# Moving the last stores of a long convolution's first stage to the SP queue, and two group loads behind its last direct transfers

## The chip, the cores and the metric

The kernel runs on one core of one Trainium2 chip. The metric is the time of one execution on the device in microseconds (us). Three runs took 2814.12, 2816.59 and 2818.91 us; the median is 2816.59 us.

## The reference

Three parts follow each other. The first is a long causal convolution by FFT of `u = x * v` (2 sequences of 12480 positions, 128 channels) with a filter that a small two-layer network makes from position embeddings, times `x`. The second and third are two expert layers over the 24960 rows, with hidden width 2048.

```python
h_filt = (np.maximum(pos_emb @ w1, 0.0) @ w2) * window
u = x * v
y = irfft(rfft(u, n=2*S) * rfft(h_filt, n=2*S), n=2*S)[:, :S]
x = (x * y).reshape(B * S, 128)
x = np.square(np.maximum(x @ w_in, 0)) @ w_out        # first expert layer
h = x @ w2_in;  out = (h * np.cos(h)) @ w2_out        # second expert layer
```

## The kernel before, in words

The FFT is written as two rounds of matrix products with a turned layout between them. That gives three stages.

**First stage** (`NCH` = 30 chunks, q = 0 to 29, each of two pairs i = 0, 1). SP loads chunk q in one transfer of 1360 KB (`load`, line 155) into one of five slots. PE multiplies by the first table (`pair`, line 198), ACT copies one half out (`v`, line 200), and DVE makes sum and difference into the tile `bt` (line 202). `store(q)` writes `bt` of both pairs to the DRAM tensor `Bs` (line 205), on the ACT queue: 112 rows of 12288 bytes, 1344 KB. In the same loop `decode` prepares the expert weights on DVE, ACT and POOL, from loads `wr` (line 84) on the SP queue.

**Second stage** (`NG` = 26 groups, g = 0 to 25). Group g needs 120 rows of `B2[g]`, one for each pair of spectrum lines; chunk q of the first stage makes rows 4q to 4q+3 of every group. `load2(g, a, b)` (line 134, on SP) reads rows a to b-1 of group g from `Bs`; each row is four pieces of 3072 bytes, one for each of the four values of k that belong to the group. A whole `load2(g)` has 128 rows (1536 KB). Only the `Bs` rows k = 4g to 4g+3 are read, so for groups 0 to 3 the first 16 rows of a store are enough. That is why the last stores are cut in two, `slice(0, 16)` (192 KB) and `slice(16, NP)` (1152 KB). `NB` = 3 groups have a slot at a time, and these slots are three of the five that the chunks used.

Rows of group 0 that come from the last two chunks don't go through DRAM: `direct(q)` (line 212) copies them inside SBUF with four transfers of 12 KB, each from 4 rows of `bt` to one row of `B2[0]`. Transfers n = 0, 1 need the first pair, n = 2, 3 the second.

PE starts a group with `spectrum` (line 285, tile `H`), two products with the filter part, one for each of c = 0, 1; ACT turns `H` into `hi` and `hr` (lines 288 to 292). Then come `product` (line 307, tile `Z`), the elementwise products on DVE and POOL, and the inverse products (line 342). In the order of the program PE does H(0,0), H(0,1), then Z of group 0's first half, then H(1,0) of group 1, then Z of group 0's second half, then H(1,1), and so on: the first product of group g+1 stands in the middle of group g, on PE and on ACT.

**Third stage.** The rest of the convolution and both expert layers, in 50 blocks of up to 512 rows.

Every engine and every queue takes its instructions in the order of the program, written out by hand. A DMA is issued when its data, its buffer, and one of eight completion semaphores are free; the semaphores are dealt out in turn, so a DMA also waits for the landing of the eighth DMA before it.

Of the kernel before, what the change touches and what calls it, by code (L numbers as in the profile page):

```python
# [23 lines left out]
NP = 112  # L24
NCH, CB = 30, 2
# [12 lines left out]
NB = 3  # L38
BT = 3
R = 96  # L40
# [14 lines left out]
def conv_moe(ctx, tc, t):  # L55
    nc = tc.nc
# [61 lines left out]
    def decode(n):  # L118
        for _ in range(n):
            next(steps, None)  # L120
# [6 lines left out]
    def slot(name, pool=ring, size=SLOT):  # L127
        return pool.tile([128, size], F32, tag="ld", name=name)

    def load2(g, a=0, b=128):  # L130

        if g not in B2:
            B2[g] = slot("B2").rearrange("p (k c e) -> p k c e", k=G4, c=2)
        nc.sync.dma_start(out=B2[g][a:b].rearrange("p k c e -> p k (c e)"),
                          in_=bass.AP(Bs.tensor, G4 * g * 4 * HB * 384 + 768 * a,
                                      [[768, b - a], [4 * HB * 384, G4], [1, 768]]))


    with ExitStack() as st:
# [37 lines left out]
        def prep(q, i):  # L177
            _, xt, vt, _ = ld[q]
            if i == 0:
                ut_t[q] = io.tile([NP, CB, 2, 384], F32, tag="ut", name="ut", bufs=3)  # L180
            u = ut_t[q]
            nc.gpsimd.tensor_tensor(out=u[:, i, :, 0:256], in0=xt[:, i], in1=vt[:, i], op=ALU.mult)
            hp = psM.tile([128, 2 * D], F32, tag="m", name="hp2")[0:NP].rearrange("p (a d) -> p a d", a=2)
            nc.tensor.matmul(hp, hT_t[q][:, i, :], w2b, start=True, stop=True)
            for a in range(2):
                nc.scalar.activation(u[:, i, a, 256:384], hp[:, a, :], AF.Copy, scale=win[:, q, i, a:a + 1])
# [3 lines left out]
        def pair(q, i):  # L190
            if i == 0:
                bt_t[q] = io.tile([NP, CB, 2, 2, 384], F32, tag="bt", name="bt", bufs=BT)
            u, bt = ut_t[q], bt_t[q]
            A = {}
            for a in (1, 0):
                A[a] = psA.tile([NP, 2, 512], F32, tag="A", name="A")
                for r in range(2):
                    nc.tensor.matmul(A[a][:, r, 0:384], turned(q, i, a, r), u[:, i, a, :], start=True, stop=True)
            v = wk.tile([NP, 2, 384], F32, tag="v", name="v")
            nc.scalar.activation(v, A[1][:, :, 0:384], AF.Copy)  # L200
            for c, op in ((0, ALU.add), (1, ALU.subtract)):
                nc.vector.tensor_tensor(out=bt[:, i, :, c, :], in0=A[0][:, :, 0:384], in1=v, op=op)

        def store(q, rows=slice(0, NP), eng=nc.scalar):
            eng.dma_start(out=Bs[rows, 8 * q:8 * (q + 1), :].rearrange("k x e -> k (x e)"),
                                in_=bt_t[q][rows].rearrange("k b r c e -> k (b r c e)"))

        def direct(q):

            for n in range(2 * CB):  # L210
                eng = nc.scalar if n % 2 else nc.sync
                eng.dma_start(out=B2[0][2 * CB * q + n:2 * CB * q + n + 1].rearrange("p k c e -> p (k c e)"),
                              in_=bt_t[q][0:G4, n // 2, n % 2].rearrange("k c e -> k (c e)"))

# [5 lines left out]
        def upto(kind, fn, n, end):  # L220
            while done[kind] < min(n, end):
                fn(done[kind])
                done[kind] += 1
# [4 lines left out]
        for n, (q, i) in enumerate(seq):  # L228
            lead = min(LA, n + 1) if n else 1
            upto("mlp", mlp1, (n + lead - 1) // CB + 1, NCH)  # L230
            upto("prep", lambda m: prep(*seq[m]), n + lead, len(seq))
            pair(q, i)
            upto("mlp", mlp1, (n + lead + 1) // CB + 1 if n else 1, NCH)
            if i == 0 and 0 < q < NCH - 2:
                store(q - 1)
            if i == 0 and q >= NCH - 4 and q - NCH + 4 < NB:
                load2(q - NCH + 4, 0, R)
            if i == 0 and q >= NCH - 2:
                store(q - 1, slice(0, 16))
                if q == NCH - 2:  # L240
                    load2(0, R, 2 * CB * q)
                else:
                    direct(q - 1)
                store(q - 1, slice(16, NP))
            if (q, i) == (NCH - 1, 1):
                direct(q)
                store(q, slice(0, 16))
                for g in range(1, NB):
                    load2(g, R)
                store(q, slice(16, NP))  # L250
            if i == 1:
                upto("load", load, q + LDB + 1, NCH)
            if 1 < n < WS:
                decode(2)
# [479 lines left out]
```

## Time and profile before

| | |
|---|---|
| median of three runs | 2816.59 us (2814.12 to 2818.91) |
| the profiled execution | 2814.05 us |
| its span from first to last instruction | 2812.3 us |
| PE / ACT / DVE / POOL busy in the span | 97% / 86% / 85% / 48% |
| chain that ended last | PE 80%, DVE 1%, ACT 1% |
| second stage begins on PE | at 254.19 us |

The page counts an engine as busy while it works on data; issuing DMAs, waiting and branching are not counted. The DMA share is the mean busy share of the core's 16 DMA engines. PEclk is the granted clock of TensorE as a share of full speed. `SPq` and `ACTq` are the instructions with which SP and ACT issue DMAs: their times are those of the issue, not of the transfer.

### The profile page before, as it was taken

What the parts mean: (1) busy time and instruction counts of PE and PEld (TensorE: products, weight loads), DVE (VectorE), ACT (ScalarE), POOL (GpSimd) and SP (SyncE); (2) the same over time, 40 slices, a digit from 0 to 9 for tenths busy, and PEclk for the clock granted to TensorE, in tenths of its full rate; (3) what the DMA queues carried; (4) which work ended last, traced back from release to release, by engine and by line L of the source; (5) the groups of instructions that cost most, each with busy time, mean ns of one, the idle gap of its engine ahead of it and who ended that gap; (6) DMA issues with size and microseconds to landing.
All of it is one profiled execution on the core that took longest, in us unless ns stands there. A gap on an engine that the chain in (4) does not pass through costs nothing.

```text
span 2812.3 us, 38640 instructions
## 1 busy us (share of the span) xinstructions
PE 2740.5 (97%) x11740; PEld 2107.4 (75%) x11740; DVE 2388.5 (85%) x4675; ACT 2416.4 (86%) x4292; POOL 1353.7 (48%) x1049
## 2 busy tenths in 40 slices
PE   8887999899999999999999999999999999999999
PEld 4543444788888888888888888888888888888887
DVE  5786999788888888888888888888888888888888
ACT  4444999699999999999999999999999999999998
POOL 4554888144444444444444444444444444444445
PEclk9999999999999999999999999999999999999999
DMA  9997887310101100101110001010001011001000
GB/s 376 391 391 260 275 284 253 90 29 25 31 28 31 28 29 19 32 28 31 28 31 19 29 28 31 28 31 28 20 27 32 28 32 28 23 25 32 16 9 9
DMA packets 83257, 222.53 MB, mean 79 GB/s; under 512 B 5552, under 2 KB 49160, under 8 KB 75848
## 3 DMA queue, kind: packets, MB, share of 16 engines
q1 hardware_dynamic: 78689, 177.99, 19.9%
q10 hardware_dynamic: 4359, 42.08, 3.7%
q8 instruction: 92, 1.51, 0.2%
q14 instruction: 117, 0.96, 0.1%
HBM read 140.29 MB, written 79.63 MB: 78 GB/s over the span
## 4 chain that ended last, share of the span: by engine, by line
PE 80%; DVE 1%; ACT 1%; issue 0%; DMA 0%; POOL 0%; SPq 0%; DVEq 0%; ACTq 0%; POOLq 0%
PE h L489 13%; PE h L491 13%; PE h L490 13%; PE y L505 13%; PE y L503 13%; PE y L504 13%; PE pc L455 4%; DVE g L577 0%; DVE r L562 0%; ACT k L554 0%; DMA dt<-dt 0%; DVE gh L587 0%; ACT g L534 0%; ACT c L569 0%; ACT r L528 0%
## 5 line engine op out<-in xcount | busy, mean ns | idle before, releaser
L594 POOL TENSOR_TENSOR gl<-g,gh 128x512 fp32r<-128x512 f32 (+2 forms) x800 | 1034.5, 1293 | 1279.9 <-ACT gh L585 738.4
L577 DVE TENSOR_TENSOR g<-h,c 128x512 f32<-128x512 f32 (+2 forms) x800 | 539.8, 675 | 244.9 <-ACT c L569 238.2
L489 PE MATMUL h<-zh,wh 128*128 128x512 f32 (+2 forms) x1600 | 642.8, 402 | 0.8 <-DVE zh L473 0.8
L554 ACT ACTIVATE k<-h,quarter 128x512 int32<-128x512 f32 (+2 forms) x800 | 541.7, 677 | 114.0 <-PE h L491 99.9
L505 PE MATMUL y<-gl,wh 128*128 128x512 f32 (+2 forms) x1600 | 624.8, 391 | 3.6 <-POOL gl L594 2.1
L491 PE MATMUL h<-zh,wl 128*128 128x512 f32 (+2 forms) x1600 | 623.4, 390 | 0.0
L490 PE MATMUL h<-zl,wh 128*128 128x512 f32 (+2 forms) x1600 | 623.1, 389 | 0.0
L503 PE MATMUL y<-gh,wl 128*128 128x512 f32 (+2 forms) x1600 | 622.6, 389 | 0.1
L504 PE MATMUL y<-gh,wh 128*128 128x512 f32 (+2 forms) x1600 | 622.1, 389 | 0.0
L569 ACT ACTIVATE c<-r,halfpi 128x512 f32<-128x512 f32 (+2 forms) x800 | 565.2, 706 | 2.6 <-DVE r L562 2.6
L528 ACT ACTIVATE r<-h 128x512 f32<-128x512 f32 (+2 forms) x800 | 472.0, 590 | 95.2 <-PE h L491 94.9
L548 DVE TENSOR_TENSOR gl<-g,gh 128x512 fp32r<-128x512 f32 (+2 forms) x800 | 537.5, 672 | 1.2
L562 DVE CUSTOM_DVE_ANT_0 r<-h,k 128x512 f32<-128x512 f32 (+2 forms) x800 | 537.8, 672 | 0.0
L534 ACT ACTIVATE g<-r 128x512 f32<-128x512 f32 (+2 forms) x800 | 492.2, 615 | 0.7 <-DVE gl L548 0.2
L541 DVE CAST gh<-g 128x512 fp32r<-128x512 f32 (+2 forms) x800 | 333.1, 416 | 41.2 <-ACT g L534 38.8
L505 PEld LDWEIGHTS y<-gl,wh 128*128 128x128 f32 x1600 | 301.4, 188 | 75.0 <-POOL gl L594 7.5
L503 PEld LDWEIGHTS y<-gh,wl 128*128 128x128 f32 x1600 | 301.7, 189 | 67.4 <-DVE zl L516 0.6
L491 PEld LDWEIGHTS h<-zh,wl 128*128 128x128 f32 x1600 | 302.0, 189 | 66.6
L504 PEld LDWEIGHTS y<-gh,wh 128*128 128x128 f32 x1600 | 301.6, 188 | 66.5
L489 PEld LDWEIGHTS h<-zh,wh 128*128 128x128 f32 x1600 | 302.7, 189 | 58.1 <-issue 1.0
L490 PEld LDWEIGHTS h<-zl,wh 128*128 128x128 f32 x1600 | 302.5, 189 | 56.3
L585 ACT ACTIVATE gh<-g 128x512 fp32r<-128x512 f32 (+2 forms) x400 | 246.4, 616 | 0.1
(62 smaller groups left out, 2439.4 us busy)
## 6 DMA issues: line engine op xcount, KB each, us to landing
ld<-ld SPq DMA_DIRECT2D x30, 1360.0 KB
Bs<-bt ACTq DMA_DIRECT2D x27, 1344.0 KB
B<-Bs SPq DMA_DIRECT2D x23, 1536.0 KB
Ds<-dt SPq DMA_DIRECT2D x26, 960.0 KB
dt<-Ds SPq DMA_DIRECT2D x59, 416.0 KB
xt<-xT SPq DMA_DIRECT2D x60, 208.0 KB
out<-o SPq DMA_DIRECT2D x47, 256.0 KB
tt<-T SPq DMA_DIRECT2D x60, 169.0 KB
```

Of the source, the lines that this page charges most:

```text
L489: nc.tensor.matmul(h[:, :n], wh[:, f, :], zh[:, :n], start=True, stop=False)
L490: nc.tensor.matmul(h[:, :n], wh[:, f, :], zl[:, :n], start=False, stop=False)
L491: nc.tensor.matmul(h[:, :n], wl[:, f, :], zh[:, :n], start=False, stop=True)
L503: nc.tensor.matmul(y[:, :n], wl[:, f, :], gh[:, :n], start=a, stop=False)
L504: nc.tensor.matmul(y[:, :n], wh[:, f, :], gh[:, :n], start=False, stop=False)
L505: nc.tensor.matmul(y[:, :n], wh[:, f, :], gl[:, :n], start=False, stop=b)
L548: nc.vector.tensor_tensor(out=gl[:, :n], in0=g[:, :n], in1=gh[:, :n].bitcast(F32), op=ALU.subtract)
L554: nc.scalar.activation(k[:, :n], hp[2, u][:, :n], AF.Identity, scale=-1.0, bias=quarter)
L562: nc.vector._custom_dve(TENSOR_ADD_SAT, out=r[:, :n], in0=h[:, :n], in1=k[:, :n], s0=0.25, s1=-0.75)
L569: nc.scalar.activation(c[:, :n], r[:, :n], AF.Sin, bias=halfpi, scale=TWO_PI)
L577: nc.vector.tensor_tensor(out=g[:, :n], in0=h[:, :n], in1=c[:, :n], op=ALU.mult)
L594: nc.gpsimd.tensor_tensor(out=gl[:, :n], in0=g[:, :n], in1=gh[:, :n].bitcast(F32), op=ALU.subtract)
```

## The change

The stores of chunks 25 to 28 and the first 16 rows of chunk 29 are issued by SP and no longer by ACT. Of the groups, only group 0 is loaded early; rows 0 to 95 of groups 1 and 2 are no longer loaded at chunks 27 and 28. After the last `direct`, group 1 is loaded as rows 0 to 115 and rows 116 to 127, and group 2 in one piece. The transfers of `direct(28)` are all on SP; those of `direct(29)` alternate between SP and ACT as before. Rows 96 to 111 of group 0 are loaded one pair later, at (28, 1), and `direct(28)` stands ahead of the stores of chunk 28.

```diff
         def direct(q):
             for n in range(2 * CB):
-                eng = nc.scalar if n % 2 else nc.sync
+                eng = nc.scalar if q == NCH - 1 and n % 2 else nc.sync
...
-            if i == 0 and 0 < q < NCH - 2:
+            if i == 0 and 0 < q < NCH - 4:
                 store(q - 1)
-            if i == 0 and q >= NCH - 4 and q - NCH + 4 < NB:
-                load2(q - NCH + 4, 0, R)
+            if i == 0 and NCH - 4 <= q < NCH - 2:
+                store(q - 1, eng=nc.sync)
+                if q == NCH - 4:
+                    load2(0, 0, R)
             if i == 0 and q >= NCH - 2:
-                store(q - 1, slice(0, 16))
-                if q == NCH - 2:
-                    load2(0, R, 2 * CB * q)
-                else:
+                if q == NCH - 1:
                     direct(q - 1)
-                store(q - 1, slice(16, NP))
+                store(q - 1, slice(0, 16), nc.sync)
+                store(q - 1, slice(16, NP), nc.sync)
+            if (q, i) == (NCH - 2, 1):
+                load2(0, R, 2 * CB * q)
             if (q, i) == (NCH - 1, 1):
                 direct(q)
-                store(q, slice(0, 16))
-                for g in range(1, NB):
-                    load2(g, R)
+                store(q, slice(0, 16), nc.sync)
+                load2(1, 0, 2 * CB * q)
+                load2(1, 2 * CB * q)
                 store(q, slice(16, NP))
+                for g in range(2, NB):
+                    load2(g)
```

## Rows read from the trace of the kernel before

**Rows 1.** Stages: stretch, its length, busy time (count) by engine, granted clock, DMA share, GB/s.

```profile
200.00:242.00 42.00, 37.35 (x116) 20.90 (x116) 36.31 (x48) 17.28 (x35) 19.65 (x15) 0.96 0.99 362
242.00:254.00 12.00, 0.48 (x2) 0.00 (x0) 2.16 (x3) 0.81 (x1) 1.31 (x2) 0.73 0.84 228
300.00:450.00 150.00, 147.08 (x333) 60.61 (x332) 138.42 (x217) 138.21 (x234) 125.01 (x100) 1.00 0.88 284
600.00:700.00 100.00, 100.00 (x452) 81.89 (x451) 86.56 (x177) 91.44 (x159) 44.97 (x34) 1.00 0.08 22
```

**Rows 2.** Order of time, 225 to 300 us: start, length, engine, line, idle before and its releaser.

```profile
234.46 2.23 PEld L198 LDWEIGHTS A<-ut,ld 112*112 112x112 f32 x8 [0.35 <-POOL ut L182]
236.12 0.81 ACT L200 ACTIVATE v<-A 112x768 f32<-112x768 f32 x1 [1.78 <-PE A L198]
...
238.20 1.81 DVE L202 TENSOR_TENSOR bt<-A,v 112x768 f32<-112x768 f32 x2
239.63 2.22 PEld L198 LDWEIGHTS A<-ut,ld 112*112 112x112 f32 x8 [0.36 <-issue]
240.53 1.82 DVE L202 TENSOR_TENSOR bt<-A,v 112x768 f32<-112x768 f32 x2
243.43 0.81 ACT L200 ACTIVATE v<-A 112x768 f32<-112x768 f32 x1 [3.91 <-DMA Bs<-bt]
244.27 1.82 DVE L202 TENSOR_TENSOR bt<-A,v 112x768 f32<-112x768 f32 x2 [1.93 <-ACT v L200]
254.19 3.73 PE L285 MATMUL H<-B,Gt 120*128 120x512 f32 x4 [11.71 <-DMA B<-bt]
262.24 1.13 PE L285 MATMUL H<-B,Gt 120*128 120x512 f32 x2 [2.60 <-ACT hr L292]
265.88 0.59 ACT L288 ACTIVATE hi<-H 64x512 f32<-64x512 f32 x1
271.87 1.02 PE L285 MATMUL H<-B,Gt 120*128 120x512 f32 x2
```

**Rows 3.** DMA issues in order of time, SP's and ACT's, each from its own stretch.

```profile
218.16 21.26 SPq L134 DMA_DIRECT2D B<-Bs  x4
239.12 0.30 SPq L134 DMA_DIRECT2D B<-Bs  x1
239.51 0.75 SPq L212 DMA_DIRECT2D B<-bt  x1
250.91 1.25 ACTq L212 DMA_DIRECT2D B<-bt  x2
252.21 0.92 ACTq L205 DMA_DIRECT2D Bs<-bt  x2
256.24 1.94 SPq L134 DMA_DIRECT2D B<-Bs  x2
```

**Rows 4.** Waits of the SP queue, 180 to 300 us: total, times, longest.

```profile
SPq L212 <- DMA B<-Bs: 7.6, 2, 4.3
```

**Rows 5.** DMA packets, 268 to 274.1 us: one whole `load2` of 128 rows alone.

```profile
DMA packets 529, 1.59 MB, mean 261 GB/s; under 512 B 16, under 2 KB 16, under 8 KB 528
q1 hardware_dynamic: 528, 1.57, 75.4%
```

**Rows 6.** DMA packets, 493 to 496.57 us: the end of one store of 120 rows.

```profile
DMA packets 174, 0.66 MB, mean 185 GB/s; under 512 B 15, under 2 KB 15, under 8 KB 172
```

**Rows 7.** DMA packets, 532 to 535.04 us: one load `tt` of 104 rows alone.

```profile
DMA packets 117, 0.17 MB, mean 57 GB/s; under 512 B 13, under 2 KB 117, under 8 KB 117
```

**Rows 8.** DMA packets, 252.2 to 252.95 us: direct transfers of 4 pieces.

```profile
DMA packets 8, 0.01 MB, mean 16 GB/s; under 512 B 4, under 2 KB 4, under 8 KB 8
```

**Rows 9.** DMA queue SP, 271 to 273 us: pieces of 3072 bytes, steady.

```profile
q1 hardware_dynamic: 272, 0.84, 102.8%
```

**Rows 10.** DMA queue SP, 243 to 245 us: pieces of 3072 bytes, crowded.

```profile
q1 hardware_dynamic: 145, 0.44, 100.3%
```

**Rows 11.** DMA queue ACT, 256 to 257 us: pieces of 12288 bytes of a store.

```profile
q10 hardware_dynamic: 32, 0.39, 109.7%
```

## The prediction

> **What bounds the kernel now.** I read the table of stages first, then the order of time around the border of stage one, then the DMA issues and SP's waits, and last the DMA packets of single transfers, because the change is about what the DMA engines do in which order.
>
> The stages have different limits [rows 1]. From 200 to 242 us the DMA engines are busy for 0.99 of the time, and no compute engine reaches 0.9. From 300 to 450 ACT (138.2 of 150) and PE (147.1) are nearly full, and the DMA engines have room. From 600 on PE is busy without a gap. So time gained or lost between stages one and two is not won back or hidden later: it goes to the end, one to one. The border itself is 242 to 254: 12 us in which PE works 0.48 us.
>
> Why 12 us? The last `bt` is ready at 244.27 + 1.82 = 246.09, and PE starts H(0,0) at 254.19 on the landing of a `direct` [rows 2]. Between them stands DMA queueing: the last two directs are issued by ACT from 250.91 to 252.16 [rows 3], not at 246.1; SP's directs waited 7.6 us for `B<-Bs` loads to land [rows 4]. Four such loads are issued between 218.16 and 239.42 [rows 3]; two of them are the early rows of groups 1 and 2, 1152 KB each. The last `v` also came late: it waited 3.91 us behind a store whose issue ACT could not finish before an earlier store had landed [rows 2].
>
> **The change, part by part.**
>
> *ACT loses its stores.* A `v` starts 236.12 - 234.46 = 1.66 us after PE's first weight load of its pair. For the last pair that gives 239.63 + 1.66 = 241.3 in place of 243.43. Then DVE is the next limit: it ends the `bt` before at 240.53 + 1.82 = 242.35, so the last one runs 242.4 to 244.2 in place of 246.09 [rows 2]. Gain 1.9 us.
>
> *The early loads of groups 1 and 2 go.* With them goes the wait of the directs for their landing. But SP now issues in one line: rows 96 to 111 of group 0 (after the first part of store 27), four directs at 0.75 us, the second two not before their `bt` at 238.20 + 1.81 = 240.0, the two parts of store 28, then two directs of chunk 29. The two waiting for 240.0 end at 241.4; the first part of store 28 goes out there, the second at 241.7. A small store took 256.24 - 252.21 = 4.0 us until the load that needs it was issued [rows 3], so it lands at 245.4. The second part has 96 rows, 6 for each engine; one row takes 1.097 x 16 / 32 = 0.55 us [rows 11], together 3.3 us. If it begins to move 1 us before the first part's landing is known (my estimate, from 0), it is through at 244.4 + 3.3 = 247.7.
>
> *The directs of chunk 29* are issued from 244.2 on (last `bt`), all four by 244.9. In the trace 2.6 us passed from the issue of the last direct, 251.6, to PE's start [rows 2, 3]; that alone would give 247.5. Two of the four stand on SP's queue behind store 28, through at 247.7; with about 1 us for landing and start, PE begins at 248.7. I take 248.5, which is 5.7 us earlier than 254.19; bounds 246.8 and 250.
>
> [...]
>
> *Group 1 is loaded late, and in an odd number of rows.* This is the step that decides. H(1,0) stands in PE's line after the first Z of group 0, and `hi` of group 1 in ACT's line. Before, PE reached it at 262.24, and ACT used it at 265.88, 265.88 - 254.19 = 11.7 us after the start [rows 2]. Started at 248.5, ACT comes to it at 260.2. By then rows 0 to 115 of group 1 must have landed.
>
> How fast are 116 rows? Each transfer closes with one small packet on each DMA engine that took part, and these are the packets under 512 bytes: 16 for a load of 128 rows [rows 5], 15 for 120 rows [rows 6], 13 for 104 rows [rows 7], 4 for a direct of 4 pieces [rows 8]. Each is the largest number up to 16 that divides the count of rows. For 116 = 4 x 29 that is 4. So I take 4 engines, each with 29 x 4 = 116 pieces of 3072 bytes. The nearest row counts, 104 and 120, ran on 13 and 15; on 15 engines each would have some 31 pieces. Those are the two ends, and I take 4 because the pattern fits all four rows.
>
> [...]
>
> One piece takes 1.028 x 16 x 2 / 272 = 0.121 us when the queue runs steadily [rows 9], 0.754 x 16 x 6.1 / 512 = 0.144 over a whole lone load with its start [rows 5], and 1.003 x 16 x 2 / 145 = 0.221 in the crowded stretch [rows 10]. With four engines asking instead of 16 I take the steady one: 116 x 0.121 = 14.0 us. The load is issued at 245.4 (it needs the first part of store 28) and moves on these engines when the store and the directs are through, at 248.1. The rest of store 29, on ACT's queue, shares them: 6 rows x 0.46 to 0.55, say 2.8 us. End: 248.1 + 14.0 + 2.8 = 264.9. Landing and start on PE 1 us, and H(1,0) at 1.9 us, because PE has stood idle again and runs slow: four products took 3.73 us at 254.19 after the long wait, two took 1.13 at 262.24 [rows 2]. ACT gets its first `hi` of group 1 at 267.8; before it was 265.88. Net: 1.9 us later.
>
> *Group 2 in one piece* follows on the same queue. Its 32 pieces for each engine take 3.9 us, so the four slow engines end at about 269. Before, H(2,0) came 271.87 - 262.24 = 9.6 us after H(1,0) [rows 2]; from 265.9 that is 275.5. Hidden, with 6 us to spare. The rows 96 to 111 of group 0 one pair later and store 25 and 26 on SP cost nothing: the DMA engines are full either way, and the load of group 0 is needed only with the last direct.
>
> *The sum*: -5.7 us at the start of stage two, and all of it plus 1.9 us is lost again in a new wait for group 1. Against the profiled execution's own 2814.05 us that is 2816.0; the median of the runs is 2.5 us above that execution, so 2818.5 on the median's scale. Bounds of the unknown: without the store in its way -2.8 + 1.9 = -0.9; at 0.144 us a piece 2.7 more, +4.6. Own range of the forecast 2815.5 to 2821.5.
>
> **The rivals.**
>
> *A. The load of 116 rows is spread over nearly all engines.* For it: 104 and 120 rows were. Then it takes about 32 pieces and lands before 256, group 1 is no wait, and the 5.7 us stay: 2816.6 - 5.7 = 2810.9. Against it: the pattern of small packets.
>
> *B. Slower than before: the four engines read at a crowded price.* The mechanism is the same new wait, with pieces that take longer, because their reads of DRAM meet the rest of store 29 and group 2. At 0.165 us a piece the price is 116 x 0.044 = 5.1 us more, 7.0 in all: 2823.6; at 0.221 it is 11.6 more, 2830.1. It decides from (5.6 - 1.9) / 116 = 0.032 above the steady price, 0.153 us, where the loss passes 0.2%. For it: the crowded stretch. Against: there 16 engines read at once, here four.
>
> *C. The directs gain nothing.* SP's single line holds them behind a store's landing, and PE starts as late as before or 2 us earlier; group 1's load then starts 3 to 4 us later too: +5.4, 2822. Against: the only landings in SP's line are those of store 27 and of the first part of store 28, and the second comes behind the directs.
>
> **How the numbers follow.** Forecast 0.62, A 0.13, B 0.17, C 0.08. About 0.2%, 5.6 us, is what a measurement can tell from no change: below 2811.0 faster, above 2822.2 slower. Faster: half of A (0.065) and an earlier start together with a cheap load, 0.065; 0.13. Slower: most of B (0.15), half of C (0.04) and the upper end of the forecast (0.07); 0.26. The same: 0.61. Range 2811 to 2825: it takes in A's time and the near half of B, and leaves out B beyond 0.18 us a piece.
>
> **What would show it.** In the trace after: the last `bt` ends near 244.2; PE's first `H` is at 247 to 250; then a second gap on PE of about 10 us, ended by `B<-Bs`; in that gap a DMA share near a quarter; 4 small packets at the end of the load of 116 rows. If PE has no second gap, the forecast is wrong and A holds. If the gap ends beyond 270, B. If the first `H` is later than 252, C. If stage three shifts against stage two by more than a microsecond, the claim that the border goes to the end one to one is wrong.

## The result, and the profile after

The changed kernel takes 2833.54 us (median of 4 runs, 2829.77 to 2837.3) against 2815.59 us for the kernel before beside it (now four runs): a ratio of 1.0061 (1.0049 to 1.0074), the medians 17.95 us apart. Forecast were 2818.5 us and a range up to 2825. The profiled execution took 2829.77 us, its span is 2828.0 us, 15.7 us longer than before.

The stages of the kernel after (stretch, length, busy time by engine, granted clock, DMA share, GB/s), to be read beside [rows 1]:

```profile
200.00:242.00 42.00, 36.04 (x117) 20.13 (x116) 37.34 (x51) 18.44 (x37) 20.57 (x16) 1.00 0.92 334
242.00:256.00 14.00, 0.01 (x1) 0.04 (x1) 0.59 (x1) 0.00 (x0) 0.00 (x0) 0.55 0.66 186
263.00:271.00 8.00, 0.00 (x0) 0.00 (x0) 2.78 (x5) 1.82 (x4) 3.75 (x3) 0.56 1.01 205
272.00:276.00 4.00, 0.00 (x0) 0.00 (x0) 0.00 (x0) 0.00 (x0) 0.00 (x0) 0.50 0.26 98
300.00:450.00 150.00, 145.00 (x333) 61.06 (x334) 138.71 (x218) 137.17 (x233) 125.44 (x101) 1.00 0.88 281
```

There are two holes now where there was one: 242 to 256, as before, and a new one up to 279.5. From 272 to 276 no engine works at all and the DMA share is 0.26, four engines of sixteen.

The order of time of the kernel after, for [rows 2, 3]:

```profile
239.46 0.81 ACT L200 ACTIVATE v<-A 112x768 f32<-112x768 f32 x1 [1.76 <-PE A L198]
240.77 1.82 DVE L202 TENSOR_TENSOR bt<-A,v 112x768 f32<-112x768 f32 x2 [0.18 <-PE A L198]
242.78 0.79 SPq L205 DMA_DIRECT2D Bs<-bt  x2
243.27 1.32 ACTq L205 DMA_DIRECT2D Bs<-bt  x1
247.44 2.69 SPq L212 DMA_DIRECT2D B<-bt  x2
255.27 0.31 SPq L205 DMA_DIRECT2D Bs<-bt  x1
255.75 36.51 SPq L134 DMA_DIRECT2D B<-Bs  x5
255.99 3.75 PE L289 MATMUL H<-B,Gt 120*128 120x512 f32 x4 [15.32 <-DMA B<-bt]
258.82 0.59 ACT L292 ACTIVATE hi<-H 64x512 f32<-64x512 f32 x1 [18.55 <-DMA Bs<-bt]
279.53 2.04 PE L289 MATMUL H<-B,Gt 120*128 120x512 f32 x2 [17.63 <-DMA B<-Bs]
281.61 0.59 ACT L292 ACTIVATE hi<-H 64x512 f32<-64x512 f32 x1 [16.74 <-PE H L289]
```

The last `bt` ends at 242.59. SP's two directs of chunk 29 go out from 247.44, the first 16 rows of store 29 (the second `SPq L205`) only at 255.27, the load of 116 rows at 255.75. PE starts H(0,0) at 255.99, 1.8 us later than before, and H(1,0) at 279.53 on the landing of group 1's rows (116 rows landed at 278.59, the other 12 at 279.40). ACT's first `hi` of group 1 starts at 281.61 in place of 265.88: 15.7 us later, which is the whole difference of the spans.

What SP waited for in the kernel after, 210 to 300 us (total, times, longest), for [rows 4]:

```profile
SPq L205 <- DMA Bs<-bt: 5.1, 1, 5.1
SPq L212 <- DMA B<-bt: 3.8, 1, 3.8
```

The 7.6 us for `B<-Bs` of [rows 4] are gone; two other waits stand in their place. Both are for completion semaphores. SP's first direct of chunk 29 has the semaphore (101 in the trace) of a direct that ACT issued at 242.62; that one landed at 247.37, and SP went on at 247.44. The first part of store 29 has the semaphore (104) of the second part, which ACT had issued early, at 243.27. That part stood in the DMA queues with store 28, landed at 255.25, and SP went on at 255.27.

One more row, of the kernel before, that the prediction left aside (ACT, order of time):

```profile
259.79 0.59 ACT L288 ACTIVATE hi<-H 64x512 f32<-64x512 f32 x1 [15.55 <-PE Z L307]
```

The row names Z, but H was ready near 256, and store 29 landed at 259.53, 0.26 us ahead of this `hi`. After, store 29 landed at 258.43, and `hi` followed at 258.82, where the row names the store. So ACT's first `hi` waits for the landing of the last store: stage two's tiles lie in memory that stage one's `bt` tiles had. Call this the gate; the kernels without it, below, show it.

### The profile page after: what moved, and what is told of

Same layout as the page of the kernel before. It is cut to its first block, busy times and chain, and to the rows that moved or that the text cites. A ratio compares the mean times of both kernels' runs of the same rounds, so it can differ in the third digit from the quotient of the medians.

```text
span 2828.0 us, 38636 instructions
## 1 busy us (share of the span) xinstructions
PE 2737.2 (97%) x11740; PEld 2107.3 (75%) x11740; DVE 2388.3 (84%) x4675; ACT 2414.8 (85%) x4292; POOL 1351.5 (48%) x1049
## 4 chain that ended last, share of the span: by engine, by line
PE 79%; DVE 1%; ACT 1%; issue 0%; DMA 0%; POOL 0%; POOLq 0%; DVEq 0%; ACTq 0%
PE h L493 13%; PE h L495 13%; PE h L494 13%; PE y L509 13%; PE y L507 13%; PE y L508 13%; PE pc L459 4%; DVE g L581 0%; ACT k L558 0%; DVE r L566 0%; DMA dt<-dt 0%; DVE gh L591 0%; ACT c L573 0%; ACT g L538 0%; ACT r L532 0%
```

## The experiments

Where ACT starts `hi` of group 1 decides what is lost or won at the border: the span minus that start is 2545.8 to 2547.7 us in before, after and the nine kernels below that leave the pools of tiles alone and cut no later group. The last `bt` ends between 240 and 254 in these profiled executions, and differs by up to 6 us between kernels that are the same up to there (group2_held 240.07, mid112 246.39), so I also give the time from there to that `hi`. Loads are told by issue and landing in the traces:

```
kernel              group 1: rows, issued, landed   us     hi(1,0)  after last bt
before              32 (rest)  256.24  262.07      5.8     265.88   19.8
after               116        255.75  278.59     22.8     281.61   39.0
rows112             112        255.90  266.19     10.3     269.31   26.6
group2_held         116        249.76  273.09     23.3     281.05   41.0
tail_store_last     116        248.04  272.13     24.1     285.46   42.8
directs_on_act      116        252.50  285.26     32.8     287.95   40.1
tail_store_mid      116        249.65  277.32     27.7     280.12   35.9
mid112              112        251.76  267.09     15.3     270.15   23.8
late_groups_only    112        251.08  262.57     11.5     269.98   19.6
stores_on_sp_only   32 (rest)  262.61  266.49      3.9     269.65   24.6
```

**The count of rows.** The kernel after, but group 1 cut at 112 = 16 x 7 rows:

```diff
-                load2(1, 0, 2 * CB * q)
-                load2(1, 2 * CB * q)
+                load2(1, 0, NP)
+                load2(1, NP)
```

> The changed kernel, group 1 loaded as rows 0 to 111 and 112 to 127 in place of 0 to 115 and 116 to 127; nothing else moves. Theory (a load of 116 rows runs on 4 of the 16 engines, one of 112 rows on 16): the load issued at about 255.8 lands in 6 to 7 us, not in 22.9; PE's H(1,0) is no longer waited for, the second gap on PE of 17.6 us is gone; what stays is the 1.8 us by which stage two starts later than before: 2817 to 2818 against 2815.6 of before. Rival (group 1 is late because everything around it is crowded, whatever its shape): the load still takes over 15 us, time over 2826.

Measured: 2820.84 us, ratio 1.0019 (1.0007 to 1.0031). The order of time of this kernel:

```profile
267.23 2.05 PE L289 MATMUL H<-B,Gt 120*128 120x512 f32 x2 [5.57 <-DMA B<-Bs]
269.31 0.59 ACT L292 ACTIVATE hi<-H 64x512 f32<-64x512 f32 x1 [4.22 <-PE H L289]
```

The load is issued at the same moment (255.90 against 255.75), four rows less are moved, and it takes 10.3 us in place of 22.8. Of the loss of 0.61%, 0.42% or 12 us go with four rows. The rest, 0.19%, has another cause; the experiments on single parts of the change, below, bear on it.

**Crowding by group 2.** The kernel after, but group 2's load waits for group 1's rows:

```diff
+                held = io.tile([1, 8], F32, tag="held", name="held", bufs=1)
+                nc.sync.dma_start(out=held, in_=B2[1][0:1, 0, 0, 0:8])
                 for g in range(2, NB):
                     load2(g)
```

> The changed kernel with a transfer of 32 bytes from row 0 of group 1 into a spare tile ahead of group 2's load, so that SP issues group 2 only when group 1's 116 rows have landed. Theory (group 2's pieces on all 16 engines crowd the reads and slow group 1's four engines from 0.127 to about 0.24 us a piece): group 1's load takes 116 x 0.127 = 14.8 us of moving, lands some 5 us earlier; time 4 to 6 us below the changed kernel. Rival (the four engines are slow by themselves): the load still takes 22 us, time the same as the changed kernel or slower by the later group 2.

Measured: 2834.98 us, 1.0060 (1.0043 to 1.0077). With group 2 out of the way the load still took 23.3 us, as the rival had it, so crowding by group 2 does not by itself make the loss. Until 253.17 the load stood beside stores. Behind that it was alone; SP's DMA queue (packets, MB, share of 16 engines), 259 to 262 and 263 to 268:

```profile
q1 hardware_dynamic: 68, 0.21, 25.3%
...
q1 hardware_dynamic: 135, 0.41, 25.7%
```

A piece took 0.253 x 16 x 3 / 68 = 0.179 and 0.257 x 16 x 5 / 135 = 0.152 us, with nothing beside it. (The added tile also held ACT's first `hi`, until 274.97, so the time of this kernel says nothing about the load.)

**The tail of store 29 behind the group loads**, on SP:

```diff
-                store(q, slice(16, NP))
                 for g in range(2, NB):
                     load2(g)
+                store(q, slice(16, NP), nc.sync)
```

> The changed kernel with the last store of chunk 29 (rows 16 to 111) moved from ACT to SP, behind group 2's load. Theory (this store, issued by ACT at 243.3 ahead of SP's last directs, holds SP's queue and these directs up): PE's first H comes at 250 to 251 in place of 255.99, group 1's load is issued 5 to 6 us earlier, still on 4 engines: time 5 to 8 us below the changed kernel, 2823 to 2828. Rival (the directs are late because they stand behind store 28 on SP's own queue, whoever issues the other store): first H stays at 254 or later, time over 2830.

Measured: 2837.86 us, 1.0070 (1.0055 to 1.0085). Its order of time:

```profile
249.96 3.75 PE L289 MATMUL H<-B,Gt 120*128 120x512 f32 x4 [9.26 <-DMA B<-bt]
255.46 6.27 SPq L205 DMA_DIRECT2D Bs<-bt  x1
279.37 0.59 ACT L292 ACTIVATE hi<-H 64x512 f32<-64x512 f32 x1 [39.06 <-DMA Bs<-bt]
```

This run showed the gate. PE's start came 6 us earlier and the load went out at 248.04, as the tail was neither in the queues ahead of SP's directs nor on the semaphore that SP's line needs (this run does not part the two); but the tail landed at 279.19 and ACT began 0.18 us later. The earlier start of PE was worth nothing here, and the expected gain of 5 to 8 us did not come.

**All directs of chunk 29 on ACT:**

```diff
-                eng = nc.scalar if q == NCH - 1 and n % 2 else nc.sync
+                eng = nc.scalar if q == NCH - 1 else nc.sync
```

> The changed kernel with all four directs of chunk 29 on ACT's queue. Theory (SP's two directs of chunk 29 are held by a completion semaphore that an ACT direct has, then stand behind store 28 in SP's queue): first H at about 248.5, the load of group 1 some 6 to 7 us earlier and still 22 us long: time 5 to 8 us below the changed kernel, 2824 to 2828. Rival (landing of directs is slow on any queue while store 28 moves): first H at 253 or later, time as the changed kernel, 2830 or more.

Measured: 2835.06 us, 1.0055 (1.0039 to 1.0071). PE started 4.8 us after the last `bt` (252.58 against 247.8) where the kernel after needs 13.4: the directs were held in SP's line. The expected gain did not come, because the 116 rows, now beside store 28 and 29, took 32.8 us.

**The tail of store 29 on SP ahead of the group loads**, with 116 rows (tail_store_mid), and the same with group 1 cut at 112 as in rows112 (mid112):

```diff
                 store(q, slice(0, 16), nc.sync)
+                store(q, slice(16, NP), nc.sync)
                 load2(1, 0, 2 * CB * q)
                 load2(1, 2 * CB * q)
-                store(q, slice(16, NP))
```

> The changed kernel with the last store of chunk 29 (rows 16 to 111) on SP, between the store of its rows 0 to 15 and the load of group 1 (still 116 rows on 4 engines). Theory: two things meet in the changed kernel beside the row count. SP's line waits for a completion semaphore that this store has when ACT issues it early (group 1's load then goes out at 255.8 in place of about 248), and ACT's first `hi` waits until the last store has landed, because stage two's tiles take the memory of stage one's. With the store here both are short: PE's first H at about 250, first `hi` at about 254, group 1's load issued at 248 to 249, landing about 270; time 6 to 9 us below the changed kernel, 2822 to 2826. Rival (only the row count matters): 2831 or more.

> tail_store_mid with group 1 loaded as rows 0 to 111 and 112 to 127. Theory (row count, SP's line and the wait for the last store are the three causes, and with all three short the change gains what it was to gain): first H at about 250, first `hi` at about 254, group 1 landed by 258 to 259, no second gap above 2 us; ACT's `hi` of group 1 at 260 to 261 against 265.88: time 3 to 6 us below before, 2810 to 2813. Rival (late loading of group 1 is a loss in itself): 2818 or more, as rows112.

Measured: 2831.76 us, 1.0062 (1.0047 to 1.0077), and 2818.66 us, 1.0009 (1.0000 to 1.0019). The first issues the 116 rows 6 us earlier than the kernel after, PE starts at 251.11, and the time stays. The pair gives the price of the count a second time: 0.53%, 15 us. But mid112 was expected at 2810 to 2813, and its rival's figure came true, 2818 or more. Its 112 rows went out at 251.76 and landed only at 267.09, with the DMA engines full (share 1.03 from 259 to 266), and PE waited for group 1:

```profile
268.07 2.05 PE L289 MATMUL H<-B,Gt 120*128 120x512 f32 x2 [8.74 <-DMA B<-Bs]
```

**One part of the change alone**, on the kernel before: the late groups (with 112 rows, stores as before), and the stores on SP (groups loaded early as before):

```diff
-            if i == 0 and q >= NCH - 4 and q - NCH + 4 < NB:
-                load2(q - NCH + 4, 0, R)
+            if i == 0 and q == NCH - 4:
+                load2(0, 0, R)
...
-                for g in range(1, NB):
-                    load2(g, R)
+                load2(1, 0, NP)
+                load2(1, NP)
                 store(q, slice(16, NP))
+                for g in range(2, NB):
+                    load2(g)
```

> The kernel before with one half of the change: groups 1 and 2 are loaded only behind the last directs (group 1 as rows 0 to 111 and 112 to 127, group 2 whole, behind the last store), all stores stay on ACT. Theory: taking away the 2.3 MB of early loads lets the directs of chunk 29 go 5 to 6 us earlier, and the last store too; first H at 248 to 249, first `hi` at about 253: time 4 to 7 us below before, 2809 to 2812. Rival (group 1 late costs what the directs gain): 2814 to 2818.

```diff
-                store(q - 1, slice(16, NP))
+                store(q - 1, slice(16, NP), nc.sync)
...
-                store(q, slice(0, 16))
+                store(q, slice(0, 16), nc.sync)
```

(and in the same way the other stores of chunks 25 to 28)

> The kernel before with the other half of the change: the stores of chunks 25 to 28 and the first 16 rows of chunk 29 on SP, the early loads of all three groups and the place of the directs as before. Theory (stores on SP stand in one line with the early loads and hold the directs up, they gain nothing by themselves): first H 0 to 4 us later, time 2815 to 2820. Rival (ACT's freedom alone is a gain): 2812 or less.

Measured: late_groups_only 2816.85 us, 1.0010 (1.0001 to 1.0020); stores_on_sp_only 2818.30 us, 1.0014 (1.0004 to 1.0023). The late groups alone cost 2.8 us, with an interval that begins near nothing (0.3), and its trace shows no loss from the last `bt` to `hi` of group 1 (19.6 us against 19.8): with 112 rows they come nearly free. The gain of 4 to 7 us that was expected did not come either. PE's first H does come sooner, 4.2 us after the last `bt` in place of 8.1, but the gate takes that back; the last store landed at 263.57:

```profile
263.90 0.59 ACT L290 ACTIVATE hi<-H 64x512 f32<-64x512 f32 x1 [15.38 <-DMA Bs<-bt]
```

The stores on SP cost 4 us: in that kernel PE's first H comes 16.4 us after the last `bt` (before: 8.1). The two small parts of the change, the later load of rows 96 to 111 of group 0 and the place of `direct(28)`, were not tried alone.

**The gate.** The `bt` tiles, and stage two's `w` and `p1`, get pools of their own, so that ACT's first tiles do not lie where the last store reads:

```diff
+        btp = st.enter_context(tc.tile_pool(name="bt1", bufs=BT, side="right"))
...
-                bt_t[q] = io.tile([NP, CB, 2, 2, 384], F32, tag="bt", name="bt", bufs=BT)
+                bt_t[q] = btp.tile([NP, CB, 2, 2, 384], F32, tag="bt", name="bt", bufs=BT)
...
+        wr2 = st.enter_context(tc.tile_pool(name="wr2", bufs=3, side="right"))
...
-                w = wk.tile([128, 2, 2, D], F32, tag="w", name="w")
+                w = wr2.tile([128, 2, 2, D], F32, tag="w", name="w")
```

(also `p1` into `wr2`, `hk2` opened ahead of `wk2`, and `dt` moved into `wk2`). It was put on the kernel before, on late_groups_only, and on l1_early. The last is late_groups_only with rows 0 to 111 of group 1 loaded ahead of `direct(28)`:

```diff
                 else:
+                    load2(1, 0, NP)
                     direct(q - 1)
...
-                load2(1, 0, NP)
                 load2(1, NP)
```

> The kernel before, with the memory of stage one's bt tiles in a pool of its own, and stage two's w and p1 in another pool, so that no tile which ACT writes first in stage two lies where the last store still reads. Theory (gate): in the kernel before, ACT's first hi starts 0.3 us after the last store lands (259.5), about 3.5 us after its H is done. Without the gate the first hi starts about 2 us after PE's first H, near 256; H of group 1 is then held by its own rows (landed 262.1) and starts near 262.5, hi of group 1 near 264.3 in place of 265.9: 1 to 2 us faster than before, about 2814 against 2815.6. Rival (PE): the first hi waits for PE or for the Z products as the page's row says, and the pools change nothing: first hi again at 259 to 260, time unchanged. Second rival: hi moves, but something after it takes up the gain, and the end minus hi of group 1 is no longer 2546 us.

> late_groups_only (groups 1 and 2 loaded behind the last direct transfers, group 1 as 112 and 16 rows, stores as in before) with the pools of before_ungated. Theory: there the first hi waited for the last store (263.9, store landed 263.6) although group 1's rows had landed at 262.6. Without the gate hi of group 1 is held by its rows alone: near 265 where it was 270, so 3 to 5 us less than late_groups_only, 2812 to 2814. Rival: the last store is not the gate, and nothing changes: 2816.9.

> The kernel before, with rows 0 to 111 of group 1 loaded in one piece just ahead of the direct transfers of chunk 28, group 2 behind the last store, the tail of the stores on ACT as before, and the gate of the last store still there. Theory (gate and load together): group 1's load has landed long before, so only the gate is left: first hi 0.3 us behind the landing of the last store, hi of group 1 about 6.1 us after it. If the store lands at 259.5 as before, the time is that of before within 1 us (2815). Rival (load alone): hi of group 1 was held by its own load alone, and with the load early it comes 3 us or more earlier: 2812 or less.

> l1_early with the pools of before_ungated: neither the last store nor group 1's own rows can hold ACT. Theory: the first hi follows PE's first H by about 2 us (H at 253 to 254, hi at 256), hi of group 1 follows by 6 us at 262, which is 3 to 5 us earlier than before: 2811, between 2809 and 2813, and faster than both kernels. Rival (something else is late): the early load of group 1 delays the direct transfers, or the last store and group 2 crowd the DMA engines so that PE's first H comes later by as much; then 2814 to 2817.

Measured, against 2817.07 us of before on this chip: before_ungated 2815.32 (0.9992, 0.9982 to 1.0002), late_groups_ungated 2814.20 (0.9993, 0.9984 to 1.0001), l1_early 2816.04 (1.0000, 0.9989 to 1.0011), l1_early_ungated 2811.28 (0.9983, 0.9975 to 0.9992). ACT's first `hi` in l1_early, with the gate:

```profile
266.89 0.59 ACT L290 ACTIVATE hi<-H 64x512 f32<-64x512 f32 x1 [15.11 <-DMA B<-Bs]
```

and in l1_early_ungated, without it, with H and `hi` of group 1:

```profile
257.25 0.59 ACT L292 ACTIVATE hi<-H 64x512 f32<-64x512 f32 x1 [10.71 <-PE H L289]
262.99 2.05 PE L289 MATMUL H<-B,Gt 120*128 120x512 f32 x2 [2.07 <-DMA B<-Bs]
265.07 0.59 ACT L292 ACTIVATE hi<-H 64x512 f32<-64x512 f32 x1 [1.77 <-PE H L289]
```

With the gate the first `hi` starts 0.33 us after the store's landing (266.56) and 5.9 us after PE's first H. (Its row names a load; the two under way landed at 267.57 and 273.21, after `hi` had begun.) Without it, 2.15 us after H (255.10), while the store lands at 261.82. In before_ungated it starts at 257.90, ahead of the landing at 261.00. So the gate is real. In time, an early load alone is worth nothing (l1_early), the new pools alone about 2 us, with an interval that holds nothing too, and both together 4.8 us (2.3 to 7.0): that version is faster than both kernels. late_groups_ungated came out where it was expected, near 2814. How much of these gains is the gate's is not shown: from the last `bt` to the end of the span the traces have 2566.2 us before, 2566.8 in before_ungated, 2566.5 in late_groups_ungated and 2565.2 in l1_early_ungated, a gain of 1.0 us at most. The rest lies ahead of the last `bt`, where the new pools move `bt` too, or between executions. My figure of 262 for `hi` of group 1 was missed: H is now held by group 1's last 16 rows, landed at 262.86. And in the three ungated kernels the span after that `hi` is 2548.2 to 2548.7 us, some 2 us more than with the old pools; why stays open.

**The price of a row count by itself.** The kernel before, with five later groups cut in two:

```diff
-                load2(seq[n][0] + NB)
+                g = seq[n][0] + NB
+                cut = {3: 116, 8: 116, 12: 120, 16: 112, 20: 118}.get(g, 128)
+                load2(g, 0, cut)
+                if cut < 128:
+                    load2(g, cut)
```

> The kernel before, with five of the later group loads of stage two cut in two: group 3 as 116 and 12 rows (issued near 268, where the DMA engines are nearly idle), group 8 as 116 and 12, group 12 as 120 and 8, group 16 as 112 and 16, group 20 as 118 and 10 (beside the stream of weights). Nothing waits for them within 9 us, so only the transfers are read. Theory (the engines alone): the 116 rows of group 3 move on 4 engines, 116 pieces each at 0.121 to 0.127 us, and land 16 to 19 us after the issue (a whole load of 128 rows takes 6.3 there); beside the stream 20 to 25 us, and 118 rows (2 engines) over 28 us, while 112 and 120 rows land within 12 us. Rival (four engines are slow by themselves): 116 rows take 22 us or more in the quiet stretch too, 0.17 us a piece, as in the changed kernel. Rival (only the border of the stages): 116 rows cost no more than 112 here, and the 23 us of the changed kernel came from stores that were just written.

Measured: 2874.01 us against 2820.65 beside it, one run each. From issue to landing:

```
rows   116 (quiet)   116   112   120   118   whole 128 before, quiet / later
us     23.5          25.3  11.3  12.1  38.3  6.3 / 9.2 to 10.5
```

(The expectation has a stream of weights beside the later loads. There is none: from 320 to 400 us SP's queue has only group loads and the stores `Ds` of stage two.)

PE's waits for them in the order of time:

```profile
294.79 2.05 PE L285 MATMUL H<-B,Gt 120*128 120x512 f32 x2 [11.63 <-DMA B<-Bs]
354.88 2.04 PE L285 MATMUL H<-B,Gt 120*128 120x512 f32 x2 [12.23 <-DMA B<-Bs]
490.54 2.05 PE L285 MATMUL H<-B,Gt 120*128 120x512 f32 x2 [26.08 <-DMA B<-Bs]
```

I had counted on 9 us in which nothing would wait for them, so that only the transfers are read. The loads took longer than that, and PE waited three times, 49.9 us in all, nearly the whole 53 us lost: for the two loads of 116 rows and the one of 118, for neither 112 nor 120. SP's DMA queue (packets, MB, share of 16 engines), 274 to 276, 281 to 284 and 460 to 464:

```profile
q1 hardware_dynamic: 63, 0.19, 25.0%
...
q1 hardware_dynamic: 229, 0.70, 103.5%
...
q1 hardware_dynamic: 64, 0.20, 12.7%
```

116 rows hold 25.0% of sixteen engines, which is four; 118 rows 12.7%, two. Alone, a piece takes 0.250 x 16 x 2 / 63 = 0.127 us here, and 0.127 x 16 x 4 / 64 = 0.127 on two engines as well. When the next whole load joins, at 281, it is 1.035 x 16 x 3 / 229 = 0.217. The border of the stages is not needed for the loss, as 116 rows are slow here too: that rival falls. The other, that four engines are slow by themselves, does not. The quiet load was expected at 16 to 19 us and took 23.5, which is the rival's figure of 22 or more. Part of that is company: the next group's load was issued at 278.89, and a piece then took 0.217 us. But group2_held had 0.152 to 0.179 us a piece with nothing beside it. Why four engines alone take 0.127 us in one stretch and 0.179 in another, and 0.144 is the figure when a whole load moves alone [rows 5], stays open.

## Why the prediction was wrong

The step that failed is SP's line of issues at the border: PE's start was put at 248.5 and the load of group 1 at 245.4, and they came at 255.99 and 255.75. Of the 13.7 us by which the load landed late, 10.4 are this step. Two smaller ones failed beside it: the price of the load on four engines, and the 11.7 us from PE's start to `hi` of group 1.

*ACT loses its stores*: right. The last `v` waited for PE's product and no longer for a store, and the last `bt` followed it. It ended 3.5 us earlier than before where I had 1.9, but that end moves by more between kernels that are the same up to there.

*The early loads of groups 1 and 2 go* and *The directs of chunk 29*: wrong, 248.5 forecast, 255.99 measured. I counted SP's landings as data waits only. The two waits that appeared, 3.8 and 5.1 us, are for completion semaphores of DMAs that ACT had issued early. The second of them fell on the first part of store 29, which stands ahead of group 1's load in SP's line and is missing from my list of that line. The 7.6 us of [rows 4] could have told me: those two directs read nothing that the early loads of groups 1 and 2 write; they had the semaphores of these loads, which landed at 243.52 and 248.48, and SP issued them at 243.59 and 248.54. Freeing ACT let its part of store 29 out at 243.27 (before: 252.69), into the queues ahead of SP's directs: those landed at 255.08 and 255.43, 7.5 us after their issue, where I had 2.6. With that part out of the way (tail_store_last, tail_store_mid) PE started 7.3 and 6.9 us after the last `bt`, with the directs on ACT (directs_on_act) 4.8, against 13.4. What moved here was the issue, by waits of 3.8 and 5.1 us; I should have asked whose landing each issue waits for. The 1 us that I put for landing and start was an estimate of mine that no run shows: PE started 0.56 us after the last direct had landed (255.43), and H(1,0) 0.13 us after the last rows of group 1 (279.40).

*Group 1 is loaded late, and in an odd number of rows*: the mechanism right, and decisive, the size wrong (22.8 us from issue to landing, forecast 19.5). Four engines it was: in row_counts 116 rows have a share of 25.0%, four of sixteen, and 118 rows 12.7%, two. The kernel after has 32 packets under 512 bytes from 258.45 to 283.2, as many as 4 + 12 + 16 for its loads of 116, 12 and 128 rows. The two pairs of kernels put 12 and 15 us on the count. The queue of SP in the kernel after, 259 to 262 and 263 to 271:

```profile
q1 hardware_dynamic: 96, 0.29, 25.4%
...
q1 hardware_dynamic: 541, 1.63, 100.4%
```

A piece took 0.254 x 16 x 3 / 96 = 0.127 us alone there, near my 0.121 (group2_held: up to 0.179), and 1.004 x 16 x 8 / 541 = 0.238 with group 2 beside. I had the load issued at 245.4 and ended at 264.9; it was issued at 255.75 and ended at 278.59. Of the 13.7 us between the two ends 10.4 are the issue and 3.3 the transfer. `hi` of group 1 was forecast at 267.8 and came at 281.61: the same 13.8 us. But the share of the issue is arithmetic, not a cure: issued 6 to 8 us earlier (tail_store_mid, tail_store_last), the load took 24 to 28 us beside the stores, and the kernels were no faster. With 116 rows nothing helped; with 112 the loss shrank to a third.

*265.88 - 254.19 = 11.7*, the time from PE's start to `hi` of group 1: wrong step, hidden by the size of the other. It is the landing of the last store (259.53) plus 6.35 us, not a chain from PE's start. tail_store_last showed it. So a start 5.7 us earlier was not a gain of 5.7 us by itself. In the kernel after, had group 1 been in time, ACT would have come to it at 258.82 + 6.1 = 264.9, 1 us earlier than before. Rival A's price was wrong for that reason too.

*Group 2 in one piece* was not hidden free of charge: its pieces shared the four engines. But in group2_held, with group 2 away, the load was no shorter. *One to one to the end*: right, 2546.4 us after `hi` of group 1 in both kernels.

*The rivals.* B's price (four engines, 0.221 at the upper end) and C's place (SP's single line, behind landings) were both right in part, and they do not exclude each other: they add. I gave each its chance alone, and so the range ended at 2825; C's 2822 - 2818.5 = 3.5 us on top of B's 2823.6 to 2830.1 would have been 2827 to 2834, and 2833.54 was measured. That this sum fits is partly luck: the trace puts 10.4 us on C's place, where C had 3.5, and 3.3 on B's, where B had 5.1 to 11.6. What is left over beside the count of rows, 4 to 5 us in rows112 and stores_on_sp_only, fits C: with the stores back on ACT (late_groups_only) 2.8 us are left, but its interval overlaps that of rows112. And the range, said to take in A's time, begins at 2811, 0.1 us above A's 2810.9.

## What to carry to other kernels

Factor the row count of every DMA that a change introduces: from issue to landing 116 rows took about twice as long as 112, 118 rows 3.4 times, and a load on four engines took 22.8 to 32.8 us wherever it was put. Before a DMA moves to another queue, list which completion semaphore it takes and who holds that; a queue freed early can hold the one that decides (here for 5.1 us). And where a stage opens, look for the last reader of the memory that its first tiles take: a wait between two landmarks of compute may really be a store's landing.

## What the runs showed of the hardware beyond that

A DMA on few engines delays the whole loads behind it: in row_counts the next whole load took 19.6 to 22.6 us in place of 6.3 to 10.5, and in the kernel after group 2's took 20.9 us (262.29 to 283.20). And the second gap slowed PE beyond its own length: with PE idle, the granted clock from 272 to 276 of the kernel after was 0.50, and the two products of H(1,0) right behind it took 2.04 us, at a granted clock of still 0.50 from 279 to 282, against 1.13 in [rows 2], at 1.00 from 261.5 to 264.
